# A planned attention and gating kernel: port-exclusive planning, output weights' words in PSUM, and batch 1's sums of v by matmuls

## The chip, the cores and the metric

The kernel runs on one core of one Trainium2 chip. The metric is the device time of one execution in microseconds (us). Times of the kernel before are 701.80, 700.61 and 698.42 us in three runs, with a median of 700.61 us.

The core has five engines that work side by side, each through its own list of instructions in a fixed order: TensorE (PE, matmuls; PEld is its loading of weights), VectorE (DVE), ScalarE (ACT), GpSimd (POOL) and SyncE (SP), which here only issues transfers. SBUF is the working memory. PSUM holds the results of matmuls; the kernel uses it as two score tiles (`sc`, 1024 floats a partition) and four banks of 512 floats (`acc`).

## The reference

Two stages, the second on the output of the first.

```python
# stage 1: B=4, H=8, S=768, D=64, 16 clusters
q_assign = argmax(q_n @ c_n)          # normalized, per head; the same for k
scores = where(q_assign == k_assign, q @ k.T / 8, -1e9)
attn = softmax(scores); x = attn @ v  # heads side by side: x is (4, 768, 512)
# stage 2: d_ff = 1024, halves u and v
h = relu(x @ w_in); u, v = h[..., :512], h[..., 512:]
v_n = (v - mean(v)) / sqrt(var(v) + 1e-6)
v_s = w_spatial @ v_n + b_spatial[:, None]
out = (u * v_s) @ w_out
```

`w_in` and `w_out` arrive as 64-bit floats. The kernel loads them as pairs of 32-bit words and puts a 32-bit float together from each pair with shifts and masks.

## The kernel before, in words

**Precision.** Products run in fp16 with a high and a low part of each operand, so that three matmuls stand for one: high by high, high by low, low by high. The high part is a scaled copy (mostly ACT), the low part a subtraction (DVE or POOL).

**Tiling.** Two heads make a pair; there are four pairs in each of four batches, so 16 pairs, n = 0 to 15. A batch's four pairs are followed by its gating stage.

- `prep(n)` loads q, k (`raw`) and v (`vraw`), forms `hq` (high parts, L532) and `lo` (low parts, L534), the logits against the centroids (L549 to L551), the one-hot assignments (L562 to L574), which a DMA transposes (`oht`, L580) and four DMAs put into `hq` as extra rows (L596), the high and low parts of v (`vhl`, L597 and L598), and the sums of v over the sequence, whose two rows go to `mean` (L622 to L626). For batch 0 (n < 4) the sums come from twelve matmuls of `ones` with `vhl` (L605, L606); for the others from a reduction of `vraw` on VectorE (L613) and a small fp32 matmul (L614).
- `shifts(n)` takes, per head, the largest score of each query: score matmuls into an `acc` bank (L654), a maximum over each (L661), then `nl` (L672), three columns on ACT (L673, L676), a DMA transpose `sht` (L677) and a DMA that puts three rows into `hq` (L678).
- `attend(n)` runs, for each of 12 tiles (6 a head), the scores (L698, L700), the exponential (L704), its fp16 copy (L706), its low part on POOL (L707) and 18 matmuls with v (L712). At a head's end the sum is divided (L731 to L733) and split into two parts (L735 on ACT, L736 on POOL).
- `mlp(b)` has six tiles of v (12 matmuls with `w_in`, ReLU on ACT at L777, mean and variance at L783 to L794, normalized at L796 to L798), six of u (L807), six products with `w_spatial` (18 matmuls, then L817 to L819 and a DMA transpose `gT`) and six with `w_out` (12 matmuls, L827). All these matmuls are issued at L756.
- The weights are converted once. `w_in` goes early, in eight jobs of 512 columns; its words are put together in `acc` banks, since its `tops` argument is that ring. `w_spatial` (12 jobs, plain fp32) and `w_out` (8 jobs of 256 columns) go later, when `w_in` is done. The words of `w_out` are put together in an SBUF tile `top` by three DVE instructions (L477, L478, L479); then come a high part on ACT (L461) and a low part on DVE (L462).

**What sets the order.** No order is written by hand. `Plan.op` collects every operation with its engine, a cost in us, what it depends on and a key. `Plan.run` then plays the program through with these costs. It always takes the engine that can start soonest, and on it, among the operations that are ready by then, the one with the smallest due time plus key. In that order the instructions are written into each engine's list. A ring (`Ring`) hands out buffers in turn, or, for `acc` and `sc`, by which comes free first. The numbers at the top of the file (`DUE`, `W_KEY`, `K_SC` and so on) are due times and keys. They take part in nothing but this choice.

Of the kernel before, what the change touches and what calls it, by code (L numbers as in the profile page):

```python
# [7 lines left out]
F32 = mybir.dt.float32  # L8
# [7 lines left out]
P = 128  # L16
# [4 lines left out]
P_LOG = 10  # L21
# [19 lines left out]
DUE_0 = 41.19  # L41
DUE = 25.06
DUE_PREP = -1.8
DUE_MAX = -0.66
DUE_M = 36.0
DUE_W = 1.18
# [6 lines left out]
W_KEY = 5.9  # L53
WL_KEY = 1.71
WL_AT = 183.82
WL_GAP = 3.25
W_AT = 31.81
W_GAP = 5.28
PREP_KEY = 2.74
AV_KEY = 0.83  # L60
K_SC = -2.21
K_MX = -3.21
K_MAX = -0.23

# [56 lines left out]
class Op:  # L121
    __slots__ = ("eng", "cost", "fn", "after", "order", "new", "claim", "key", "at", "dma", "turn", "cols", "due", "left", "ready", "outs", "end", "seq", "alt", "s", "free")
# [7 lines left out]
OVER = {"PE": 0.0, "ACT": 0.1, "DVE": 0.083, "POOL": 0.04, "SP": 0.0, "NONE": 0.0}  # L130

# [5 lines left out]
class Plan:  # L137
# [12 lines left out]
    def op(self, eng, cost, fn, after=(), use=(), new=(), claim=(), key=0.0, at=0.0, dma=None, turn=False, cols=0, alt=None, due=None):  # L150
        o = Op()
        o.due = self.due if due is None else due
# [9 lines left out]
    def run(self):  # L162
# [19 lines left out]
        hw = [0.0, 0.0]  # L182
        lanes = []
# [26 lines left out]
        while done < len(self.ops):  # L210
# [29 lines left out]
            if o.dma is None:  # L240
# [11 lines left out]
                o.end = s + c  # L252
                free[e] = o.end - OVER[e]
# [22 lines left out]
def kernel(  # L276
# [76 lines left out]
    r_top = R(wk, "top", [P, 256], F32, 1)  # L353
# [49 lines left out]
    def fill():  # L403
# [4 lines left out]
    c_wt = op("DVE", 1.2, fill, key=-8)  # L408
    c_id = op("DVE", 0.2, lambda: V.tensor_copy(out=id16, in_=idt()), after=[ld_i], use=[scratch], key=0)
    c_z = op("DVE", 0.5, lambda: (V.memset(cmh, 0.0), V.memset(cml, 0.0)), key=-8)  # L410
    c_oh = op("POOL", 1.0, lambda: (G_.memset(ohx, 0.0), G_.memset(ohx.rearrange("p t (x e) c -> p t x (e c)", e=2)[:, :, 0:2, C:C + 1], PEN)), key=-8)
    c_sh = op("POOL", 2.0, lambda: [G_.memset(x, 0.0) for x in shx], key=-7)
    c_mean = op("POOL", 0.6, lambda: [G_.memset(x, 0.0) for x in mean], key=-6)
    c_wh = op("POOL", 0.5, lambda: (G_.memset(one32, 1.0), [G_.memset(x[:, :, D:D + 1], S * MEAN_UNIT) for x in whs], [G_.memset(x[:, :, D:D + 1], 0.0) for x in wls]), key=-5)
    c_one = op("POOL", 0.8, lambda: [G_.memset(x[:, :, :, D:D + 1], 1.0) for x in vhl], key=-9)
    o = chain("DVE", [
        (0.1, lambda: V.tensor_tensor(out=sq(), in0=cn(0), in1=cn(0), op=ALU.mult)),
        (0.1, lambda: V.tensor_reduce(out=ss, in_=sq(), axis=AX.X, op=ALU.add)),
# [21 lines left out]
    c_cm = op("DVE", 1.0, place_c, after=[o, c_z], use=[ct], key=KC)  # L440
# [11 lines left out]
    def weights(jobs, at, gap, key, raws, tops, on, after=()):  # L452
        ends = []
        for m, (src, dst, n, lg, wide, cell) in enumerate(jobs):
# [4 lines left out]
            def lows(x, ld, n=n, dst=dst, sc=sc, raw=raw, cell=cell, use=()):  # L459

                h = op("ACT", 0.2 + 0.00085 * n, lambda: A.activation(out=dst()[:, 0, :], in_=x(), func=AF.Copy, scale=sc), after=ld, use=use, key=key)  # L461
                lo = op("DVE", (0.05 if n > 384 else 0.4) + 0.00125 * n, lambda: V.scalar_tensor_tensor(out=dst()[:, 1, :], in0=x(), scalar=sc, in1=dst()[:, 0, :], op0=ALU.mult, op1=ALU.subtract), after=[h], use=use, key=key)  # L462
                w_ops.setdefault(cell, []).extend([h, lo])
                ends.append(lo)
# [434 lines left out]
```

## Time and profile before

| what | value |
|---|---|
| times of three runs | 701.80, 700.61, 698.42 us |
| span of the profiled execution, first to last instruction | 696.3 us |
| median of the runs less that span | 4.3 us |
| mean granted TensorE clock | 0.993 |
| PE busy | 632.9 us, 91% |
| DVE busy | 480.1 us, 69% |
| ACT busy | 431.6 us, 62% |
| POOL busy | 427.4 us, 61% |

The page gives no time of the profiled execution's own beside its span, so the median less the span stands for what lies around it. Busy time is the time in which at least one instruction of an engine ran. Instructions of one engine overlap a little, and the ends of matmuls are modelled, so a busy PE is not a PE at its peak. "Idle before" in a row is the idle time of the engine just before such instructions, with what ended it. Lines are those of the kernel before; the changed file has the same code four lines lower from L355 on.

### The profile page before, as it was taken

The numbers are of one execution on the slowest core, as the hardware profiler recorded it, in microseconds if no ns is written. First come the engines' busy times: TensorE is split into PE (matmuls) and PEld (weight loads), VectorE is DVE, ScalarE is ACT, GpSimd is POOL, SyncE is SP. The second block draws the span as 40 slices with busy tenths as digits, with TensorE's granted clock in tenths as the row PEclk, the third lists the DMA queues.
The fourth block names the chain that finished last, engine by engine and source line by source line (L and its number), as shares of the span: only waits on it lengthen the run. The fifth ranks groups of instructions, "written<-read, shape, count | busy, mean of one in ns | idle before, by whom it ended". The sixth has DMA issues, their size and how long they took to land.

```text
span 696.3 us, 16724 instructions
## 1 busy us (share of the span) xinstructions
PE 632.9 (91%) x6751; PEld 374.0 (54%) x6751; DVE 480.1 (69%) x945; ACT 431.6 (62%) x679; POOL 427.4 (61%) x301
## 2 busy tenths in 40 slices
PE   2578789989899798999999999999999899989996
PEld 1245556656545455556555656556655556544442
DVE  6979999998976999978496858557586812015210
ACT  2359899988856856748773848558664855522111
POOL 1038698998756856847666857758575967613210
PEclk9999999999999999999999999999999999999999
DMA  5585664857342658283532437446410122230123
GB/s 163 138 220 129 176 151 89 166 123 143 87 126 61 141 151 183 69 194 73 150 76 54 108 46 120 105 107 106 112 30 1 37 43 54 49 96 1 31 60 91
DMA packets 107321, 70.69 MB, mean 102 GB/s; under 512 B 91182, under 2 KB 93932, under 8 KB 107244
## 3 DMA queue, kind: packets, MB, share of 16 engines
q1 hardware_dynamic: 103500, 62.94, 40.8%
q10 hardware_dynamic: 3744, 6.69, 2.8%
q8 instruction: 53, 0.87, 0.5%
q14 instruction: 24, 0.20, 0.1%
HBM read 27.63 MB, written 6.29 MB: 49 GB/s over the span
## 4 chain that ended last, share of the span: by engine, by line
PE 60%; DVE 24%; ACT 6%; DMA 6%; issue 3%; POOL 1%; SPq 0%; ACTq 0%; DVEq 0%; POOLq 0%
PE acc L756 35%; DVE nm L661 10%; PE acc L712 10%; PE sc L698 5%; PE sc L700 5%; PE acc L654 4%; ACT p L704 2%; ACT pt L706 2%; DMA gT<-ghl 2%; DMA sht<-shx 1%; DMA raw<-in_kqT_dram 1%; DVE lo L534 1%; DVE vhl L598 1%; POOL pt L707 1%; DVE wsp L462 1%
## 5 line engine op out<-in xcount | busy, mean ns | idle before, releaser
L707 POOL TENSOR_TENSOR pt<-p,pt 128x768 f16<-128x768 f32 x192 | 325.1, 1710 | 110.7 <-ACT pt L706 86.9
L704 ACT ACTIVATE p<-sc,plog 128x768 f32<-128x768 f32 x192 | 169.2, 898 | 43.4 <-PE sc L700 39.5
L661 DVE TENSOR_REDUCE nm<-acc 128x1 f32<-128x512 f32 (+1 forms) x288 | 178.7, 682 | 5.2 <-PE acc L654 4.9
L706 ACT CAST pt<-p 128x768 f16<-128x768 f32 x192 | 155.6, 830 | 7.6 <-PE acc L712 5.9
L712 PEld LDWEIGHTS <-pt 128*128 128x128 f16 x3456 | 125.6, 98 | 27.5 <-POOL pt L707 7.7
L712 PE MATMUL acc<-vhl,pt 128*128 128x65 f16 (+1 forms) x3456 | 134.6, 194 | 6.2 <-POOL pt L707 6.0
L756 PE MATMUL acc<-win,xT 128*128 128x512 f16 x576 | 130.0, 380 | 0.0
L654 PE MATMUL acc<-hq 80*128 80x256 f16 (+1 forms) x384 | 101.2, 338 | 19.0 <-DVE nm L661 10.1
L698 PE MATMUL sc<-hq,lo 128*128 128x512 f16 (+1 forms) x384 | 95.8, 331 | 6.4 <-ACT p L704 6.2
L700 PE MATMUL sc<-hq 81*128 81x512 f16 (+1 forms) x384 | 96.1, 332 | 4.4 <-DMA hq<-sht 4.4
L756 PE MATMUL acc<-vn,wsp 128*128 128x512 f16 x432 | 97.1, 379 | 0.1
L756 PEld LDWEIGHTS <-xT 128*128 128x128 f16 x576 | 55.1, 98 | 64.0 <-issue 1.7
L817 DVE SCALAR_TENSOR_TENSOR u<-acc,bsp,u 128x512 f32<-128x512 f32 x24 | 18.0, 749 | 92.3 <-PE acc L756 92.3
L819 POOL TENSOR_TENSOR ghl<-u,ghl 128x512 f16<-128x512 f32 x24 | 28.8, 1199 | 73.4 <-DVE ghl L818 65.8
L756 PE MATMUL acc<-wou,gT 128*128 128x512 f16 x288 | 65.8, 379 | 4.3 <-DMA gT<-ghl 4.3
L756 PEld LDWEIGHTS <-wsp 128*128 128x128 f16 x432 | 41.6, 98 | 48.5 <-issue 0.2
L654 PEld LDWEIGHTS <-hq 80*128 80x128 f16 x384 | 34.5, 99 | 42.0 <-issue 21.7
L700 PEld LDWEIGHTS <-hq 81*128 81x128 f16 x384 | 37.9, 99 | 31.3 <-issue 6.3
L698 PEld LDWEIGHTS <-lo 128*128 128x128 f16 x384 | 34.2, 98 | 34.7 <-issue 19.7
L534 DVE SCALAR_TENSOR_TENSOR lo<-raw,hq 128x768 f16<-128x768 f32 x32 | 41.7, 1305 | 15.7 <-ACT hq L532 15.6
L756 PEld LDWEIGHTS <-gT 128*128 128x128 f16 x288 | 27.5, 97 | 36.8 <-DMA gT<-ghl 5.8
L827 ACT ACTIVATE o<-acc 128x512 f32<-128x512 f32 x24 | 14.3, 596 | 48.9 <-PE acc L756 34.9
(104 smaller groups left out, 619.1 us busy)
## 6 DMA issues: line engine op xcount, KB each, us to landing
raw<-in_kqT_dram SPq DMA_DIRECT2D x15, 768.0 KB
vraw<-in_vp_dram SPq DMA_DIRECT2D x16, 384.0 KB
out_dram<-o ACTq DMA_DIRECT2D x24, 256.0 KB
hq<-hq SPq DMA_DIRECT2D x15, 384.0 KB
vn<-in_w_in_dram SPq DMA_DIRECT2D x8, 512.0 KB
hq<-lo SPq DMA_DIRECT2D x16, 192.0 KB
lo<-hq SPq DMA_DIRECT2D x16, 192.0 KB
wraw<-in_wsT_dram SPq DMA_DIRECT2D x12, 192.0 KB
```

Source lines behind the costliest of these rows:

```text
L534: los.append(op("DVE", 1.4 if n else 0.96, lambda h=h: V.scalar_tensor_tensor(out=lo.t[:, h, :], in0=raw.t[:, h, :], scalar=QK_SCALE, in1= ...
L654: T.matmul(out=acc.t[:, c:c + cs.stop - cs.start], lhsT=hq.t[0:R_SH, 1, h, t * P:(t + 1) * P], rhs=hq.t[0:R_SH, 0, h, cs], start=c == 0, s ...
L661: V.tensor_reduce(out=nm.t[:, t, k:k + 1] if n == 1 else nm.t[:, t:t + n, k], in_=src, axis=AX.X, op=ALU.max, negate=True)
L698: T.matmul(out=sc.t[:, cs], lhsT=lo.t[:, h, ks], rhs=hq.t[:, 2, h, cs], start=True, stop=False)
L700: T.matmul(out=sc.t[:, cs], lhsT=hq.t[0:R_E, 0, h, ks], rhs=hq.t[0:R_E, 1, h, cs], start=False, stop=True)
L704: o = op("ACT", 0.9, lambda sc=sc, p32=p32: A.activation(out=p32.t, in_=sc.t[:, 0:S], func=AF.Exp, bias=plog, scale=SC_UNIT), after=[o, m_ ...
L706: o = op("ACT", 0.83, lambda pt=pt, p32=p32: A.copy(out=pt.t[:, 0, :], in_=p32.t), after=[o], use=[p32], new=[pt], key=K_HI)
L707: o = op("POOL", 1.72, lambda pt=pt, p32=p32: G_.tensor_tensor(out=pt.t[:, 1, :], in0=p32.t, in1=pt.t[:, 0, :], op=ALU.subtract), after=[o ...
L712: T.matmul(out=av.t[:, t * (D + 1):t * (D + 1) + w], lhsT=lhsT, rhs=rhs, skip_group_check=True, **f)
L756: T.matmul(out=acc.t, lhsT=lr[m][0], rhs=lr[m][1], start=(m == 0), stop=(m == n - 1))
L817: o = op("DVE", 0.72, lambda: V.scalar_tensor_tensor(out=u32.t, in0=acc.t, scalar=bsp[:, t:t + 1], in1=u32.t, op0=ALU.add, op1=ALU.mult), ...
L819: l = op("POOL", 1.2, lambda: G_.tensor_tensor(out=ghl.t[:, 1, :], in0=u32.t, in1=ghl.t[:, 0, :], op=ALU.subtract), after=[h], use=[u32, g ...
```

## The change

Four things change.

1. **The planner gets a lock.** An operation may be marked `lock`; every POOL operation that is not a transfer is. While the plan is played, one number, `port`, holds the time until which the last locked operation runs, and a locked operation ends no sooner than that time, less 0.13, plus its cost. Marked on DVE are operations whose operands lie in SBUF alone: `lo` (L534), the copies of `hq` (L536), the low part of v (L598), the small statistics and the normalization (L789 to L797), `ghl` (L818), and the low parts of weights that come straight from `raw` (L462).
2. **Costs and keys are new.** Costs of DVE, ACT and POOL operations are other numbers (POOL's low part of the exponential 1.65 instead of 1.72, `lo` 0.94 instead of 1.4, the small statistics 0.16 instead of 0.3), and so are the due times and keys at the top. Costs, due times and keys move instructions; they change none.
3. **The words of `w_out` go to `acc` banks.** The ring `top` in SBUF is gone; `late_weights` passes `r_acc`, and a job uses the first 256 columns of a bank.
4. **The sums of v of batch 1** (n = 4 to 7) come from the twelve matmuls, as in batch 0, instead of L613 and L614.

Apart from points 3 and 4, each engine has the same instructions as before, in another order.

```diff
-DUE_0 = 41.19
-DUE = 25.06
+DUE_0 = 42.99
+DUE = 23.281
...
-DUE_M = 36.0
-DUE_W = 1.18
+DUE_M = 37.729
+DUE_W = 0.985
...
-WL_KEY = 1.71
-WL_AT = 183.82
-WL_GAP = 3.25
+WL_KEY = 5.317
+WL_AT = 181.201
+WL_GAP = -7.18
...
+PORT = 0.13
...
+        o.lock = dma is None and (lock or eng == "POOL")
...
+        port = 0.0
...
                 o.end = s + c
+                if o.lock:
+                    o.end = port = max(s, port - PORT) + c
                 free[e] = o.end - OVER[e]
...
-    r_top = R(wk, "top", [P, 256], F32, 1)
...
-            x1 = op("DVE", (0.1 if n > 256 else 0.3) + 0.0011 * n, lambda raw=raw, top=top, n=n: V.tensor_scalar(out=top.t.bitcast(U32), in0=words(raw, n, 1), scalar1=3, scalar2=0x3FFFFFFF, op0=ALU.logical_shift_left, op1=ALU.bitwise_and), after=[ld], use=[raw], new=[top], key=key)
+            x1 = op("DVE", 0.1 + 0.00113 * n, lambda raw=raw, top=top, n=n: V.tensor_scalar(out=top.t[:, 0:n].bitcast(U32), in0=words(raw, n, 1), scalar1=3, scalar2=0x3FFFFFFF, op0=ALU.logical_shift_left, op1=ALU.bitwise_and), after=[ld], use=[raw], new=[top], key=key)
...
-            lows(lambda top=top: top.t, [x3], use=[top])
+            lows(lambda top=top, n=n: top.t[:, 0:n], [x3], use=[top], lock=False)
...
-        weights(jobs, WL_AT, WL_GAP, WL_KEY, r_wraw, r_top, "SP", after)
+        weights(jobs, WL_AT, WL_GAP, WL_KEY, r_wraw, r_acc, "SP", after)
...
-        short = n >= NPR
+        short = n >= 2 * NPR
...
-                o = op("POOL", 1.72, lambda pt=pt, p32=p32: G_.tensor_tensor(out=pt.t[:, 1, :], in0=p32.t, in1=pt.t[:, 0, :], op=ALU.subtract), after=[o], use=[p32, pt], key=K_LO)
+                o = op("POOL", 1.65, lambda pt=pt, p32=p32: G_.tensor_tensor(out=pt.t[:, 1, :], in0=p32.t, in1=pt.t[:, 0, :], op=ALU.subtract), after=[o], use=[p32, pt], key=K_LO)
```

Three places show what the new plan moves. Numbers in the names tell buffers apart.

**ACT, around the 63rd to the 66th exponential (pair 5), while the gating stage of batch 0 begins.** `v` at L777 (L781 after) and `u` at L807 (L811 after) take in a tile of twelve matmuls with `w_in`. Before:

```order
L597 ACTIVATE vhl_89<-vraw 128x12x64
L704 ACTIVATE p_3013<-sc_111,plog 128x768
L704 ACTIVATE p_3042<-sc_110,plog 128x768
L706 CAST pt<-p_3013 128x768
L706 CAST pt<-p_3042 128x768
L735 CAST xhl<-xn 128x6x64
L704 ACTIVATE p_3097<-sc_111,plog 128x768
L532 ACTIVATE hq<-raw 128x768
L706 CAST pt<-p_3097 128x768
L704 ACTIVATE p_3136<-sc_110,plog 128x768
```

Now:

```order
L739 CAST xhl<-xn 128x6x64
L710 CAST pt<-p_2941 128x768
L710 CAST pt<-p_2961 128x768
L811 ACTIVATE u_3013<-acc_113 128x512
L708 ACTIVATE p_3065<-sc_111,plog 128x768
L708 ACTIVATE p_3091<-sc_110,plog 128x768
L710 CAST pt<-p_3065 128x768
L628 ACTIVATE wl_95<-w_3101 2x2x65
L710 CAST pt<-p_3091 128x768
L781 ACTIVATE v_3166<-acc_113 128x512
```

Before, the third tile with `w_in` follows the 71st exponential. Now a tile of u follows the 62nd and the third tile of v the 64th, so 24 matmuls with `w_in` stand earlier in PE's list.

**DVE, the first two jobs of `w_out`, between the shifts of pair 7 and those of pair 8.** Before:

```order
L477 TENSOR_SCALAR top<-wraw 128x256
L732 RECIPROCAL rc<-rc 128x6
L534 SCALAR_TENSOR_TENSOR lo<-raw,hq 128x768
L733 TENSOR_TENSOR xn<-acc_114,rc 128x384
L817 SCALAR_TENSOR_TENSOR u_3313<-acc_115,bsp,u_3313 128x512
L622 TENSOR_SCALAR wh_93<-acc_113 2x2x64
L478 SCALAR_TENSOR_TENSOR top<-wraw,top 128x256
L623 SCALAR_TENSOR_TENSOR w_4086<-acc_113,wh_93 2x2x64
L818 CAST ghl<-u_3313 128x512
L479 SCALAR_TENSOR_TENSOR top<-wraw,top 128x256
L462 SCALAR_TENSOR_TENSOR wou<-top,wou 128x256
L477 TENSOR_SCALAR top<-wraw 128x256
```

Now:

```order
L822 CAST ghl<-u_3013 128x512
L481 TENSOR_SCALAR acc_113<-wraw 128x256
L578 TENSOR_SCALAR ohx<-acc_115 128x6x2x16
L482 SCALAR_TENSOR_TENSOR acc_113<-wraw,acc_113 128x256
L481 TENSOR_SCALAR acc_115<-wraw 128x256
L483 SCALAR_TENSOR_TENSOR acc_113<-wraw,acc_113 128x256
L482 SCALAR_TENSOR_TENSOR acc_115<-wraw,acc_115 128x256
L538 SCALAR_TENSOR_TENSOR lo<-raw,hq 128x768
L821 SCALAR_TENSOR_TENSOR u_3416<-acc_114,bsp,u_3416 128x512
L735 TENSOR_SCALAR rc<-acc_112 128x6
L483 SCALAR_TENSOR_TENSOR acc_115<-wraw,acc_115 128x256
```

The words now stand in the banks `acc_113` and `acc_115`, and two jobs are open at once, where before one tile `top` served one job after the other.

**SP, the first shift of pair 0.** Before:

```order
L538 DMA hq<-hq 64x2x1536
L580 DMA_TRANSPOSE oht<-ohx 128x6x128
L677 DMA_TRANSPOSE sht<-shx_86 128x6x128
L472 DMA vn<-in_w_in_dram 128x1024
L596 DMA hq<-oht 17x768 x2
L678 DMA hq<-sht 3x768
L596 DMA hq<-oht 16x768 x2
```

Now:

```order
L542 DMA hq<-hq 64x2x1536
L681 DMA_TRANSPOSE sht<-shx_86 128x6x128
L584 DMA_TRANSPOSE oht<-ohx 128x6x128
L476 DMA vn<-in_w_in_dram 128x1024
L682 DMA hq<-sht 3x768
L600 DMA hq<-oht 17x768 x2
L600 DMA hq<-oht 16x768 x2
```

The transpose for pair 0's shift goes ahead of that for pair 1's one-hot rows, and its rows are written before theirs.

More of the change, by code (lines that the diff above doesn't have):

```diff
@@ L121 @@
 class Op:
-    __slots__ = ("eng", "cost", "fn", "after", "order", "new", "claim", "key", "at", "dma", "turn", "cols", "due", "left", "ready", "outs", "end", "seq", "alt", "s", "free")
+    __slots__ = ("eng", "cost", "fn", "after", "order", "new", "claim", "key", "at", "dma", "turn", "cols", "due", "left", "ready", "outs", "end", "seq", "alt", "s", "free", "lock")
 LAG = {"PE": 0.2, "ACT": 0.034, "DVE": 0.034, "POOL": 0.034, "SP": 0.0, "NONE": 0.0}
@@ L148, in ring, with op @@
         return r
-    def op(self, eng, cost, fn, after=(), use=(), new=(), claim=(), key=0.0, at=0.0, dma=None, turn=False, cols=0, alt=None, due=None):
+    def op(self, eng, cost, fn, after=(), use=(), new=(), claim=(), key=0.0, at=0.0, dma=None, turn=False, cols=0, alt=None, due=None, lock=False):
         o = Op()
+        o.lock = dma is None and (lock or eng == "POOL")
         o.due = self.due if due is None else due
@@ L438, in place_c @@
             V.tensor_tensor(out=cml[r, :, i, :], in0=ctv[r], in1=cmh[r, :, i, :], op=ALU.subtract)
-    c_cm = op("DVE", 1.0, place_c, after=[o, c_z], use=[ct], key=KC)
+    c_cm = op("DVE", 1.25, place_c, after=[o, c_z], use=[ct], key=KC)
     w_ops = {}
@@ L776, in v_tile @@
             k = t % 2
-            o = op("ACT", 0.57, lambda: A.activation(out=v32.t, in_=acc.t, func=AF.Relu, scale=2.0 ** -(X_LOG + WIN_LOG)), after=[o], use=[acc], new=[v32], key=K_VT)
+            o = op("ACT", 0.596, lambda: A.activation(out=v32.t, in_=acc.t, func=AF.Relu, scale=2.0 ** -(X_LOG + WIN_LOG)), after=[o], use=[acc], new=[v32], key=K_VT)
             if k == 0:
@@ L792, in v_tile @@
[L792 to L794 removed]
+            o = op("DVE", 0.165, lambda: V.tensor_scalar(out=a.t, in0=mv.t[:, :, 1], scalar1=1e-6, scalar2=None, op0=ALU.add), after=ags, use=[mv], new=[a], key=0, lock=True)
@@ new lines, in v_tile @@
+            o = op("POOL", 0.69, lambda: G_.tensor_tensor(out=y.t, in0=a.t, in1=mhalf.broadcast_to([P, 2]), op=ALU.pow), after=[o, m_half], use=[a], new=[y], key=-2)
+            o = op("DVE", 0.16, lambda: V.tensor_tensor(out=y2.t, in0=y.t, in1=y.t, op=ALU.mult), after=[o], use=[y], new=[y2], key=0, lock=True)
+            o = op("DVE", 0.16, lambda: V.tensor_tensor(out=y2.t, in0=y2.t, in1=a.t, op=ALU.mult), after=[o], use=[y2, a], key=0, lock=True)
+            o = op("DVE", 0.16, lambda: V.tensor_scalar(out=y2.t, in0=y2.t, scalar1=-0.5 * 2.0 ** VN_LOG, scalar2=1.5 * 2.0 ** VN_LOG, op0=ALU.mult, op1=ALU.add), after=[o], use=[y2], key=0, lock=True)
@@ L799, in v_tile @@
+                l = op("POOL", 1.25, lambda t=t, v=v: G_.tensor_tensor(out=vn[:, 1, t, :], in0=v.t, in1=vn[:, 0, t, :], op=ALU.subtract), after=[h], use=[v], key=1)
                 normed.extend([h, l])
```

130 lines of the change are left out of this document (62 added, 68 removed).

## The prediction

> **What bounds the kernel now.** First the page's sums and its chain of waits, then the windows by stage, then the waits.
>
> ```profile
> span 696.3 us, 16724 instructions
> PE 632.9 (91%) x6751; PEld 374.0 (54%) x6751; DVE 480.1 (69%) x945; ACT 431.6 (62%) x679; POOL 427.4 (61%) x301
> PE 60%; DVE 24%; ACT 6%; DMA 6%; issue 3%; POOL 1%; SPq 0%; ACTq 0%; DVEq 0%; POOLq 0%
> ```
>
> PE is the bound over the whole, and VectorE holds a quarter of the chain. Where, the windows tell (each engine's busy us in the stretch, then the granted PE clock):
>
> ```profile
> 0.00:50.00 50.00, 25.14 (x221) 13.55 (x222) 38.80 (x102) 17.84 (x29) 6.84 (x20) 1.00 0.60 166
> 50.00:125.00 75.00, 64.40 (x991) 45.74 (x988) 72.67 (x137) 68.21 (x110) 63.17 (x40) 0.98 0.60 144
> 125.00:200.00 75.00, 66.91 (x893) 43.59 (x889) 70.91 (x124) 64.49 (x101) 65.02 (x42) 0.95 0.57 121
> 200.00:300.00 100.00, 92.87 (x1033) 54.89 (x1033) 88.27 (x165) 66.64 (x111) 64.06 (x40) 1.00 0.52 128
> 300.00:600.00 300.00, 294.57 (x3163) 175.13 (x3160) 186.55 (x364) 198.59 (x306) 205.26 (x141) 1.00 0.39 82
> 600.00:696.30 96.30, 89.00 (x474) 41.10 (x472) 22.91 (x58) 15.86 (x26) 23.04 (x21) 1.00 0.22 54
> ```
>
> The columns are PE, PEld, DVE, ACT, POOL. PE is idle for 24.9 us in the first 50, 10.6 to 125, 8.1 to 200, 7.1 to 300, 5.4 in the next 300 and 7.3 at the end. VectorE is busy 72.7 of 75 us, then 70.9 of 75, then 88 of 100, and after that 187 of 300. So the time is to be won before 300 us, where VectorE is nearly full; behind that PE runs through, and a shorter VectorE buys nothing.
>
> **The change, part by part.**
>
> *Batch 1's sums by matmuls.* What goes is a reduction on VectorE and a two-pass fp32 matmul, what comes is twelve fp16 matmuls. The rows of both: grouped, the waits, a piece of the chain, and in order of time:
>
> ```profile
> L613 DVE TENSOR_REDUCE vs<-vraw 128x128 f32<-128x768 f32 x12 | 17.8, 1487 | 0.2 <-DMA vraw<-in_vp_dram 0.2
> PE acc L614 <- DVE vs L613: 3.3, 3, 1.4
> 363.85 1.37 DVE vs L613
> 73.51 0.22 PE L605 MATMUL acc<-vhl,ones 128*128 128x130 f16 x1
> 74.15 0.22 PE L606 MATMUL acc<-vhl,ones 128*128 128x128 f16 x1
> 118.86 0.38 PE L614 MATMUL acc<-vs,one 128*2 128x128 f32 x2 [0.68 <-DVE vs L613]
> 119.17 0.39 PE L654 MATMUL acc<-hq 80*128 80x512 f16 x1
> ```
>
> VectorE loses 4 x 1.49 = 5.9 us of work. PE's twelve start from 73.51 to 74.15, and one more step of 0.06 makes 0.70; L614 takes 0.31 to the next start. So PE gains 4 x (0.70 - 0.31) = 1.6 us of work. Against it stands PE's wait for the reduction: 3.3 us in three, of which the 1.4 is at 364 us, in batch 2, and stays; the 1.9 goes. Net -0.3. The new chain has to wait for the low part of v, which the reduction did not. That is covered, as pair 4 shows, the tightest case:
>
> ```profile
> 126.89 1.57 DVE L598 SCALAR_TENSOR_TENSOR vhl<-vraw,vhl 128x768 f16<-128x768 f32 x1
> 151.31 0.34 PE L712 MATMUL acc<-mean,hq 83*128 83x65 f16 x6
> ```
>
> From 128.5 to the first use at 151.3 there are 22.8 us; if that cover were gone, it would cost the 0.70 us of the matmuls and a transfer a pair. The twelve wait themselves, though, and PE keeps its order: scores queued behind them then wait for a late low part, by at most the 1.57 us that a blocked one takes. The plan places them where it expects the low part to be there, so I count nothing. The 5.9 us on VectorE I count at nothing by themselves: they lie beside PE's work and show only in the order below.
>
> *Words of the output weights in PSUM.* The SBUF words (shortest, median and longest ns, first and last start; then mean ns), one of the same instructions on `w_in`, whose words already stand in a bank, and POOL's main work:
>
> ```profile
> L477 DVE TENSOR_SCALAR top<-wraw x8: 278/298/1618, 247.5 to 298.4; 128x256 uint32<-128x256 uint32 x8
> L478 DVE SCALAR_TENSOR_TENSOR top<-wraw,top x8: 403/722/1865, 250.0 to 298.7; 128x256 uint32<-128x256 uint32 x8
> L462 DVE SCALAR_TENSOR_TENSOR wou<-top,wou x8: 403/420/1590, 252.3 to 300.9; 128x256 f16<-128x256 f32 x8
> L478 DVE SCALAR_TENSOR_TENSOR top<-wraw,top 128x256 uint32<-128x256 uint32 x8 | 7.6, 952 | 0.1
> L479 DVE SCALAR_TENSOR_TENSOR top<-wraw,top 128x256 uint32<-128x256 uint32 x8 | 7.3, 918 | 0.1
> L477 DVE TENSOR_SCALAR top<-wraw 128x256 uint32<-128x256 uint32 x8 | 5.0, 625 | 0.1
> L462 DVE SCALAR_TENSOR_TENSOR wou<-top,wou 128x256 f16<-128x256 f32 x8 | 5.6, 700 | 1.6 <-ACT wou L461 1.6
> L478 DVE SCALAR_TENSOR_TENSOR acc<-vn,acc 128x512 uint32<-128x512 uint32 x8 | 5.3, 686 | 0.0
> L707 POOL TENSOR_TENSOR pt<-p,pt 128x768 f16<-128x768 f32 x192 | 325.1, 1710 | 110.7 <-ACT pt L706 86.9
> ```
>
> In SBUF one form takes 0.40 to 1.87 us; twice the size in a bank takes 0.69 on average, so those hardly wait for anyone. POOL's low part takes 1.71 us, and the longest extra, 1865 - 403 ns, stays under that. The new price of one instruction lies between 0.40 (the free case in SBUF) and 0.69 (512 columns); I take 0.42, since the form and the size are those of the first. The four cost 625 + 952 + 918 + 700 = 3195 ns now and 4 x 0.42 = 1.68 us then: 8 x 1.5 = 12 us of VectorE less (3 us at the upper bound), between 247 and 301 us.
>
> The Trainium skill (SBUF — State Buffer, "Who interferes with whom") states that a VectorE instruction with two SBUF inputs and a GpSimd instruction that reads SBUF exclude each other for a whole instruction; the spread of L478 agrees. Its page VectorE: DVE Perf Modes ("Why PSUM operands drop a tier") speaks against the change: L477, with one input, would lose its double rate in PSUM. The 278 ns of its quickest case beside 403 for the two-input form agrees; by that rule the 12 us would be 11.
>
> What of it reaches PE? In that stretch PE waits little, and mostly for a bank that VectorE's `u` product has yet to free, queued behind such words:
>
> ```profile
> 250.00:275.00 25.00, 22.61 (x274) 13.61 (x271) 23.20 (x37) 13.17 (x22) 15.32 (x10) 1.00 0.77 189
> 275.00:300.00 25.00, 24.34 (x295) 15.13 (x293) 24.90 (x48) 19.45 (x32) 17.22 (x11) 1.00 0.39 88
> PE acc L654 <- DVE u L817: 2.3, 1, 2.3
> ```
>
> PE is idle 2.4 and 0.7 us, so 3.1 is all that can come back here. I take -2.0; the other 10 us are off the path.
>
> *The order.* Two tiles with `w_in`, 24 matmuls, move up from behind the 71st exponential. Their price and the place they move to:
>
> ```profile
> 200.34 7.88 PE acc L756 x36
> 150.00:175.00 25.00, 23.48 (x331) 15.33 (x328) 21.88 (x38) 22.89 (x37) 22.18 (x15) 1.00 0.66 133
> 175.00:200.00 25.00, 21.55 (x224) 12.89 (x220) 24.95 (x42) 18.58 (x29) 20.27 (x14) 0.86 0.36 79
> 200.00:225.00 25.00, 25.00 (x236) 13.73 (x236) 15.16 (x40) 14.07 (x26) 12.21 (x9) 1.00 0.37 110
> 225.00:250.00 25.00, 20.91 (x238) 12.42 (x236) 25.00 (x45) 19.95 (x34) 19.30 (x13) 1.00 0.54 126
> ```
>
> A matmul is 7.88 / 36 = 0.219 us, so 5.3 us of PE work leave the block from 200 us on, where PE is full (25.00) and the others idle, and go where PE is idle 1.5 + 3.5 us and its granted clock is 0.86 of full over 25 us, another 3.5 us of PE time lost. Bounds: nothing, if pair 5's scores are pushed back by as much, and 8.5 us. I take -4.5, a little over half, because exponentials, copies and POOL there stand at 22 of 25 us and cannot close up much. Between 225 and 250 PE is idle 4.1 us while VectorE is full; 5.9 us of sums are gone from VectorE by then, but the weights of `w_spatial` still lie there: -1.0 (0 to -4.1).
>
> The clock's dip comes where PE is thinly used. The Trainium skill (TensorE: Matmul & The Clock Gate, Part 1) states that after a window of some 3.4 us with too little activity the clock is halved for at least as long; the 0.86 agrees with two such windows. If the thin stretch only moves (by its list PE still has no matmuls with `w_in` among the scores of pair 5's second head), so does the dip, which is why I do not count all 3.5.
>
> *The start.* Pair 0's shift rows are written before the one-hot rows of pair 1:
>
> ```profile
> 32.20 2.07 SPq L580 DMA_TRANSPOSE oht<-ohx  x1
> 38.01 0.70 SPq L678 DMA_DIRECT2D hq<-sht  x1
> PE sc L700 <- DMA hq<-sht: 4.4, 1, 4.4
> ```
>
> PE's longest wait, 4.4 us, ends with these rows. The transpose of 2.07 us that now goes ahead will not, so the first exponential may come up to 2 us sooner. But pair 1 follows VectorE, which is full from 50 to 75 us, and its own one-hot rows are now later by as much. I take 0 (bounds -2 and +2).
>
> *The rest.* From 300 us on no engine's list loses or gains work, and from the last matmuls with v to the end PE's list is the same sequence. Moved pieces there can cost or win within the 5.4 us that PE idles: 0. The lock itself costs the chip nothing; it is a number in the planner.
>
> **The sum.** -0.3 - 2.0 - 4.5 - 1.0 = -7.8 us against the profiled span: 696.3 becomes 688.5. The median of the runs lies 4.3 above that span, and I carry the difference over: 700.6 - 7.8 = 692.8, say 693.
>
> **The rivals.**
>
> *No change.* Up to 200 us the softmax's chain of exponential, copy and POOL's low part, at 22 to 23 of 25 us, paces every pair; more matmuls among the scores push the pair back, and PE idles later instead. For it: DVE, ACT and POOL are all around 90% busy there. Against it: the block from 200 us on, in which these three are at 12 to 15 of 25, would still be shorter. Without the order's -5.5 the sum is -2.3: 698.
>
> *Slower: four banks are too few.* A job's words hold a bank from the first word to the low part. A job's bank would have been held from 247.5 to past 252.3 with the first one, and two jobs are now open at once, beside the bank that collects a head's output, one for the logits and one for a tile of the gating stage. Maxima and gating tiles then wait for a bank, PE in its fixed order with them. The price is half a tile of twelve matmuls (6 x 0.219 = 1.3 us) for each of eight jobs, 10.5 us, which replaces the -2.0: 693 + 2 + 10.5 = 705. It decides from 1.2 us a job on, where it has eaten all of the gain (9.8 / 8). For it: the 2.3 us wait above is one for a bank. Against: all of PE's waits for maxima are short, those in the stretch where `w_in`'s words held banks included:
>
> ```profile
> PE acc L654 <- DVE nm L661: 10.1, 23, 1.6
> ```
>
> *More.* PE's idle time from 125 to 300 us, 15.2 us, goes down to the share of the later 300 us (1.8%, 3.2 us), and the clock's 3.5 comes back: -15: 685.5.
>
> *The planner's lock does not catch what the chip does*, so that its order is only another order, worth as much as any: no particular sign, within 4 us of before: 700.
>
> **How the numbers follow.** What a measurement of this kernel can tell from no change is about 0.5%, 3.5 us. Forecast, 688 to 697: 0.50. More, below 688: 0.11. No change or an order like any other, 697 to 704: 0.23. Banks or another stall, above 704: 0.16. The forecast's own range is 688 to 697; that of 8 in 10 is 686 to 705, where the lower end is the case "more" and the upper one the banks at their price. Faster 0.61, same 0.23, slower 0.16.
>
> **What would show it.** Right: the words at 0.42 us each with hardly a spread; PE idle in 150 to 200 us below 3 us, with pair 6's first scores some 5 us earlier than in this row; the same PE work from 300 us on, only sooner.
>
> ```profile
> 219.38 0.49 PE L698 MATMUL sc<-hq,lo 128*128 128x512 f16 x2
> ```
>
> For the banks: waits of PE for VectorE's `u` or maxima of more than 5 us in 240 to 300. For the pace: pair 5's and pair 6's exponentials as late as now. Wrong is the forecast if the stretch from 300 us on grows by more than 3 us, or if PE's idle time before 125 us, 35.5 now, moves by as much.

## The result

The changed kernel takes 679.37 us (median of four runs, 678.34 to 679.79), the kernel before 701.16 in the same comparison (four runs, 698.42 to 701.80). The ratio is 0.970, with a 95% interval of 0.968 to 0.972: 21.8 us faster. Two further executions of the kernel before and one of a run below took over 900 us at a granted clock of 0.67; ratios, intervals and the clock's loss in this document leave them out. Forecast was 693, so the sign was right, the size was not: the time lies below the forecast's range, and below the 686 of the range of 8 in 10 too. The head of the page after, and of its chain of waits:

```profile
span 677.3 us, 16827 instructions
PE 628.3 (93%) x6791; PEld 375.3 (55%) x6791; DVE 460.5 (68%) x941; ACT 433.3 (64%) x679; POOL 423.7 (63%) x301
PE 57%; DVE 26%; ACT 6%; issue 5%; DMA 4%; POOL 2%; SPq 0%; ACTq 0%; DVEq 0%; POOLq 0%
```

The span is 19.0 us shorter; PE's busy time fell by 4.6 us, VectorE's by 19.6. Every execution on record with both numbers takes 1.7 to 1.9 us more than its span. So of the 4.3 us by which the median of the kernel before lies above its profiled span, some 2.5 only mean that the profiled execution was a quick one; that is why the two spans differ by less than the medians. The windows by stage (PE, PEld, DVE, ACT, POOL, granted PE clock):

```profile
0.00:50.00 50.00, 26.59 (x249) 14.69 (x250) 42.32 (x109) 19.37 (x31) 8.87 (x21) 1.00 0.59 164
50.00:125.00 75.00, 65.20 (x1000) 46.12 (x997) 72.82 (x136) 70.08 (x111) 63.96 (x40) 0.95 0.70 156
125.00:200.00 75.00, 72.32 (x935) 47.50 (x932) 65.63 (x129) 66.29 (x108) 66.02 (x43) 1.00 0.59 135
200.00:300.00 100.00, 95.69 (x1089) 57.81 (x1088) 79.39 (x157) 66.75 (x110) 65.14 (x43) 1.00 0.61 141
300.00:600.00 300.00, 296.67 (x3203) 177.00 (x3201) 180.56 (x363) 199.46 (x303) 203.82 (x141) 1.00 0.35 76
600.00:677.30 77.30, 71.87 (x333) 32.18 (x330) 19.81 (x51) 11.34 (x19) 15.95 (x15) 1.00 0.21 48
```

PE's idle time fell from 8.1 to 2.7 us between 125 and 200, from 7.1 to 4.3 up to 300, from 5.4 to 3.3 in the next 300 and from 7.3 to 5.4 at the end. The dips of the clock between 125 and 200 us (0.95 before) are gone; between 50 and 125 us the clock stands a little lower than before (0.95 for 0.98). The longest of what PE waits for between 50 and 310 us (waits: us in all, times, longest), before and after:

```profile
PE sc L698 <- ACT p L704: 6.2, 9, 2.0
PE acc L654 <- DVE nm L661: 5.5, 16, 1.6
PE acc L712 <- POOL pt L707: 4.9, 8, 1.5
```

```profile
PE sc L702 <- ACT p L708: 3.2, 7, 1.2
PE acc L609 <- DVE xn L737: 2.1, 1, 2.1
PE acc L658 <- DVE nm L665: 2.1, 9, 0.4
PE acc L716 <- POOL pt L711: 1.8, 3, 0.9
```

The three long lists of short waits (exponentials, maxima, POOL's low part) shrank together, from 16.6 to 7.1 us. Single longer waits came and went: the 2.3 us for `u` that the prediction shows is gone, and 2.1 us at a sum of v (L609) are new. The words of the output weights, grouped, are as forecast, 0.42 us:

```profile
L481 DVE TENSOR_SCALAR acc<-wraw 128x256 uint32<-128x256 uint32 x8 | 3.3, 415 | 0.0
L482 DVE SCALAR_TENSOR_TENSOR acc<-wraw,acc 128x256 uint32<-128x256 uint32 x8 | 3.3, 420 | 0.1
```

And pair 6's first scores, with two bursts of the values' matmuls (in order of time):

```profile
206.27 1.25 PE L716 MATMUL acc<-vhl,pt 128*128 128x65 f16 x36
...
211.03 0.49 PE L702 MATMUL sc<-hq,lo 128*128 128x512 f16 x2
...
245.81 0.70 PE L716 MATMUL acc<-vhl,pt 128*128 128x65 f16 x18
```

They start at 211.03 instead of 219.38 us: 8.4 us had been won by then, and another 11 came later. The bursts tell why busy PE hides some of that: 36 matmuls take 1.25 us, 18 take 0.70, so one more costs 0.031, and about 0.15 us at a burst's end counts as busy without a new matmul starting (an estimate from these two rows; the ends of matmuls are modelled). By it a wait shorter than that between two bursts is no idle time on the page. The Trainium skill (Perfetto Trace Analysis, "Identifying the Most-Contended Engine") states that matmul busy time is a poor measure of how near PE is to its limit, because matmuls are pipelined; the two bursts agree.

### The profile page after: what moved, and what is told of

The parts are those of the page before. It is cut to its first block, busy times and chain, and to the rows that moved or that the text cites. A ratio compares the mean times of both kernels' runs of the same rounds, so it can differ in the third digit from the quotient of the medians.

```text
span 677.3 us, 16827 instructions
## 1 busy us (share of the span) xinstructions
PE 628.3 (93%) x6791; PEld 375.3 (55%) x6791; DVE 460.5 (68%) x941; ACT 433.3 (64%) x679; POOL 423.7 (63%) x301
## 4 chain that ended last, share of the span: by engine, by line
PE 57%; DVE 26%; ACT 6%; issue 5%; DMA 4%; POOL 2%; SPq 0%; ACTq 0%; DVEq 0%; POOLq 0%
PE acc L760 33%; DVE nm L665 11%; PE acc L716 9%; PE sc L702 5%; PE sc L704 5%; PE acc L658 4%; DMA gT<-ghl 3%; ACT p L708 2%; DVE lo L538 1%; ACT pt L710 1%; DVE vhl L602 1%; DVE acc L481 1%; POOL pt L711 1%; DVE acc L482 1%; DVE acc L569 1%
## 5 line engine op out<-in xcount | busy, mean ns | idle before, releaser
L716 PE MATMUL acc<-vhl,pt 128*128 128x65 f16 (+1 forms) x3456 | 132.6, 193 | 2.1 <-POOL pt L711 1.8
L658 PE MATMUL acc<-hq 80*128 80x256 f16 (+1 forms) x384 | 98.6, 336 | 11.0 <-DVE nm L665 6.0
L538 DVE SCALAR_TENSOR_TENSOR lo<-raw,hq 128x768 f16<-128x768 f32 x32 | 44.6, 1406 | 24.2 <-ACT hq L536 24.1
L811 ACT ACTIVATE u<-acc 128x512 f32<-128x512 f32 x24 | 14.3, 597 | 56.2 <-PE acc L760 50.3
```

What stands on the lines that cost most here:

```text
L538: los.append(op("DVE", 0.94, lambda h=h: V.scalar_tensor_tensor(out=lo.t[:, h, :], in0=raw.t[:, h, :], scalar=QK_SCALE, in1=hq.t[:, 0, h, ...
L658: T.matmul(out=acc.t[:, c:c + cs.stop - cs.start], lhsT=hq.t[0:R_SH, 1, h, t * P:(t + 1) * P], rhs=hq.t[0:R_SH, 0, h, cs], start=c == 0, s ...
L716: T.matmul(out=av.t[:, t * (D + 1):t * (D + 1) + w], lhsT=lhsT, rhs=rhs, skip_group_check=True, **f)
```

## The experiments

Where a run keeps an order, the planner's choice is replaced by a list of operation numbers, and its dependences stay:

```diff
+ORDER = [0, 10, 2, 3, 6, ...]
...
-            best = None
...
+            o = self.ops[ORDER[done]]
```

Three runs keep the list strictly: the new order with the old instructions, words back in SBUF and sums back to the reduction. In the other runs that keep an order, an operation that isn't ready in the play-through, or has no free buffer there, stands back until it is, so a few operations can move.

All results in one table. "Clock's loss" is the span times one less the granted clock, the median over a run's executions: an upper bound of what dips cost, since a dip costs nothing where PE would have waited. "Without it" is the span times the clock, so a lower bound. The kernel before, run beside each of the four groups of runs that follow, had medians of 698.9, 698.8, 700.1 and 700.8 us, and 701.2 beside the changed kernel. So a difference of medians between two groups, and one to the changed kernel's 679.4, can be off by some 2 us beyond the intervals.

| run | median us | ratio to before, 95% | clock's loss | without it |
|---|---|---|---|---|
| kernel before (77 executions in the four groups) | 698.8 to 700.8 | 1 | 7.0 to 9.1 | 690 to 691 |
| changed kernel | 679.4 | 0.970 (0.968 to 0.972) | 3.4 | 674.2 |
| new order, both old instructions | 693.0 | 0.991 (0.988 to 0.994) | 10.7 | 680.3 |
| old order, both new instructions | 703.1 | 1.006 (1.004 to 1.009) | 10.5 | 690.8 |
| planned without the lock | 693.6 | 0.992 (0.989 to 0.995) | 6.2 | 686.5 |
| planned with the old keys | 702.6 | 1.004 (1.002 to 1.007) | 14.0 | 686.4 |
| words back in SBUF | 687.1 | 0.983 (0.978 to 0.988) | 8.9 | 676.4 |
| sums back to the reduction | 686.3 | 0.982 (0.977 to 0.987) | 6.2 | 679.2 |
| start undone | 680.7 | 0.974 (0.969 to 0.980) | 3.7 | 675.8 |
| tiles back | 689.5 | 0.986 (0.982 to 0.990) | 7.2 | 680.8 |
| three undone | 702.9 | 1.005 (1.002 to 1.007) | 15.4 | 685.9 |
| old order, tiles up | 703.1 | 1.006 (1.003 to 1.008) | 10.5 | 691.1 |
| old order, instructions placed | 697.9 | 0.998 (0.996 to 1.000) | 7.0 | 689.6 |
| old order, all three | 701.1 | 1.002 (1.000 to 1.005) | 9.8 | 689.4 |
| old order to pair 4, then new | 686.3 | 0.980 (0.976 to 0.984) | 4.1 | 679.8 |
| new to pair 4, then old | 697.5 | 0.996 (0.993 to 0.998) | 9.0 | 686.2 |
| new to pair 6, then old | 691.8 | 0.989 (0.985 to 0.993) | 11.0 | 679.9 |
| old to pair 8, then new | 697.8 | 0.997 (0.995 to 0.999) | 8.4 | 688.3 |

### Order and instructions apart

**New order, old instructions.** The changed kernel's order, words in SBUF (two buffers), sums by the reduction ahead of the low part of v.

```diff
+    r_top = R(wk, "top", [P, 256], F32, 2)
-        weights(jobs, WL_AT, WL_GAP, WL_KEY, r_wraw, r_acc, "SP", after)
+        weights(jobs, WL_AT, WL_GAP, WL_KEY, r_wraw, r_top, "SP", after)
-        short = n >= 2 * NPR
+        short = n >= NPR
```

> The order of the changed kernel, kept operation by operation, with the instructions of the kernel before: words of the output weights in SBUF (two buffers) and batch 1's sums by the reduction, put in front of the low part of v. Theory A (the order carries the gain, the instructions little): 679 to 685 us, at least three quarters of the 21.8 us between 701.2 and 679.4 remain. Theory B (VectorE's work, 18 us less by the rows, carries it): 692 us or more. By my sum of before, the instructions alone are worth 2.3 us, so 682.

**Old order, new instructions.** The kernel before's order, with both new instructions; the sums' matmuls stand right behind the low part of v that they need.

```diff
-        weights(jobs, WL_AT, WL_GAP, WL_KEY, r_wraw, r_top, "SP", after)
+        weights(jobs, WL_AT, WL_GAP, WL_KEY, r_wraw, r_acc, "SP", after)
-        short = n >= NPR
+        short = n >= 2 * NPR
```

> The reverse: the order of the kernel before, kept but for a few operations that a bank not yet free, or the sums' wait for the low part of v, moves back, with the words in PSUM banks and batch 1's sums by matmuls. Theory A: 696 to 702 us. Theory B: 690 us or less. If the four banks are too few in an order that was not made for them: above 703, with waits of PE for VectorE between 240 and 300 us.

**Without the lock**, and **with the old keys**: the changed kernel, planned anew.

```diff
-        o.lock = dma is None and (lock or eng == "POOL")
+        o.lock = False
```

> The changed kernel, planned anew with the lock left out of the planner; costs, due times, keys and instructions as changed. Theory A1 (the lock makes the order fit the chip): half of the gain or more is lost, 690 us or more. Theory A2 (the keys make the order, and the lock only moves planned times): 678 to 685 us.

```diff
-DUE_0 = 42.99
-DUE = 23.281
...
+DUE_0 = 41.19
+DUE = 25.06
...
```

> The changed kernel, planned anew with the due times and keys of the kernel before; lock, costs and instructions as changed. Theory A1 (lock and costs suffice): 678 to 687 us. Theory A2 (the keys make the order): 690 us or more.

The new order alone gives 5.9 us of the 21, the new instructions alone lose 4.2: they are worth 13.6 us in the new order and less than nothing in the old. A reason for the loss stands in the waits between 110 and 235 us of the old order with new instructions; the run "instructions placed" below takes it away:

```profile
PE acc L723 <- DVE vhl L715: 4.4, 3, 1.5
```

Three times PE stands 1.5 us at a sum, for the low part of v, with the next scores queued behind. In the new order with the old instructions, the clock dips where PE becomes thin (two windows, clock 0.88 and 0.87):

```profile
225.00:250.00 25.00, 23.36 (x323) 16.04 (x323) 23.74 (x43) 20.89 (x36) 20.52 (x13) 0.88 0.45 89
250.00:275.00 25.00, 20.33 (x172) 11.00 (x171) 22.95 (x39) 9.11 (x17) 10.76 (x8) 0.87 0.60 137
```

Without the lock, 14 us of the gain are lost, and with the old keys all of it. But each is another plan as a whole, one of many that such numbers give. That the lock helps because it foresees the port is not shown by this.

### One part undone in the changed kernel

**Words in SBUF** and **sums by the reduction**, each the edit above alone.

> The changed kernel with every engine's order kept, only the words of the output weights back in SBUF, with two buffers so that two jobs may still be open at once; the sums of v stay matmuls. With both old instructions this order took 693.0 us, with both new ones 679.4; this run and the next share out the 13.6 us. Theory A (the port: in SBUF the words wait for POOL and POOL for them, between 225 and 300 us, where VectorE is full): most of it comes back, 687 to 691 us, lost between 225 and 300 us, with nothing lost by pair 4's first scores (139 us). Theory B (what counted in the first run was the reduction, already before 143 us): 680 to 682 us. By the prediction's terms (2.0 for the words): 681.

> The changed kernel with every engine's order kept, only batch 1's sums of v back to one reduction on VectorE and one two-pass matmul a pair, the reduction just ahead of the low part of v; the words stay in PSUM. Theory A: VectorE has 4 x 1.5 us more before 225 us, and the run that undid both had lost 3.5 us by pair 4's first scores; the rest was the words: 682 to 684 us. Theory B: 688 to 692 us, since the delay before 143 us is handed on and grows. By the prediction's terms (0.3): 680. If the two parts add up, this run and the one with words in SBUF lose 13.6 us together; if less, each hides the other.

Words: 7.7 us slower. PE's waits from 225 to 300 us, a window there, and the second word:

```profile
PE acc L773 <- DVE u L936: 2.9, 1, 2.9
PE acc L773 <- ACT u L926: 1.7, 1, 1.7
```

```profile
250.00:275.00 25.00, 20.41 (x198) 12.27 (x197) 22.13 (x38) 14.05 (x25) 13.32 (x9) 0.93 0.60 150
```

```profile
L597 DVE SCALAR_TENSOR_TENSOR top<-wraw,top x8: 407/426/1261, 239.6 to 279.6; 128x256 uint32<-128x256 uint32 x8
```

In SBUF this word takes up to 1.26 us again (0.64 on average, by its group's row), in a bank 0.42; the rule of exclusion that the prediction cited from the Trainium skill (SBUF — State Buffer, "Who interferes with whom") agrees. The four steps of a job take 633 + 642 + 535 + 847 ns on average here and 415 + 420 + 417 + 415 in the changed kernel, so VectorE has 7.9 us more to do. VectorE's `u` comes late, PE waits 2.9 and 1.7 us for maxima tiles whose bank is not free, and the clock dips (0.93 of 25 us, 1.8 us). Before, the same wait was 2.3 us.

Sums: 7.0 us slower. PE's waits from 110 to 235 us, in this run and in the changed kernel:

```profile
PE acc L772 <- DVE nm L779: 3.3, 10, 0.7
PE acc L732 <- DVE nm L779: 2.4, 3, 1.2
```

```profile
PE acc L658 <- DVE nm L665: 1.0, 4, 0.4
```

The reduction itself is hardly waited for (0.2 us). The maxima stand behind it in VectorE's list, and PE waits for those, ten times at their own matmuls and three times at the sums' small matmul (L732). The two runs together lose 14.7 us, the run that undid both 13.6: the parts add up within the intervals, and each of theory A and B had half of it.

**The start undone.** SP's list:

```diff
-L681 hq<-sht ahead of L584 oht<-ohx (the change)
+L584 oht<-ohx and two rows of hq<-oht ahead of L681 sht and L682 hq<-sht
```

> The changed kernel with the start's two transfers back as they were: the one-hot rows of pair 1 are transposed and written before pair 0's shift rows; nothing else moves. By the prediction's term: 0, so 679 us, since pair 1 follows VectorE. By the traces of both kernels (first exponential 42.74 us before, 41.38 after, and pairs 1 to 3 earlier by 2.2 to 2.7 us): 1.4 us later at the first exponential and 1.4 to 2.7 us at the end, 681 to 682 us.

The median is 1.3 us higher, by the ratios to the kernel before 3 us (0.974 for 0.970), and the two intervals overlap. The profiled span is the same (677.2 and 677.3): pair 4's first scores come 1.2 us later (140.3 for 139.1), pair 7's second head is level (262.2 and 262.4). So the profile is with the term of 0, but the times can't tell it from the 1.4 to 2.7 us of the other reading.

**The two tiles back.**

```diff
  exponential 62
-u 0: 12 matmuls with w_in, ReLU
  exponential 64
-v 2: 12 matmuls with w_in, ReLU, statistics
  ...
  exponential 71
+u 0, v 2
```

> The changed kernel with the two tiles with w_in (24 matmuls, with their ReLU or statistics) back behind the 71st exponential, where they stood before; all else in its order. By the prediction's term for them, 4.5 us: 684 us, with PE thin between 150 and 200 us again. Rival 1 (the tiles only fill time in which PE would have waited anyway, and give no more than their own 5.3 us of PE work): at most 685. Rival 2 (the softmax's chain paces these pairs, and moving the tiles wins nothing): 679 to 680. If the thin stretch brings a dip of the clock too, up to 3.5 us more: 687.

10.1 us slower, twice the term. Two windows of this run, then of the changed kernel:

```profile
150.00:175.00 25.00, 21.81 (x318) 15.22 (x318) 18.17 (x33) 22.46 (x37) 21.77 (x15) 0.97 0.62 153
175.00:200.00 25.00, 21.54 (x195) 12.45 (x194) 15.22 (x29) 14.85 (x23) 15.23 (x11) 0.89 0.35 87
```

```profile
150.00:175.00 25.00, 24.21 (x335) 16.43 (x333) 19.08 (x35) 22.75 (x38) 22.52 (x16) 1.00 0.64 160
175.00:200.00 25.00, 24.15 (x219) 13.69 (x218) 22.32 (x49) 18.95 (x33) 18.61 (x13) 1.00 0.49 110
```

PE idles 5.0 us more (6.65 for 1.64) and loses 3.5 us to the clock (0.03 and 0.11 of 25 us): 8.5 of the 10.3 us by which pair 6's first scores are late here (221.3 for 211.0). In the new order the tiles fill time that PE would have idled, and the clock stays up with them.

### The same parts put into the old order

**Three undone** is the control: the changed order with both old instructions and the tiles back, the edits above together.

> The changed kernel's order with three parts undone at once: words in SBUF with two buffers, batch 1's sums by the reduction, and the two tiles with w_in back behind the 71st exponential. If the parts add up (13.6 us for both instructions, 10.1 for the tiles): 703 us, as slow as the kernel before, and nothing else in the order carries any gain. If the parts are paid for by the same idle time: 695 to 699.

702.9: they add up, and without them the new order gains no time. It has the largest clock's loss of all runs, though; with that set aside it stands at 685.9 us, the kernel before at 690 to 691. So the three parts looked like the whole change. The other three runs put them into the old order.

**Tiles up:** in the old order u 0 and v 2 move from behind the 71st exponential to where the change has them. Their matmuls follow the 62nd and the 64th exponential, as in the change; the ReLU of v 2 follows the 67th here (64th there), and v 1 stays behind the 62nd, where the change has it behind the 60th.

> The kernel before with its order kept and only the two tiles with w_in (24 matmuls and what follows them) moved up to where the change has them, behind the 62nd to 66th exponential. By the prediction's term, 4.5 us: 696.5. If they are worth here what moving them back cost in the changed kernel, 10.1 us: 691, with the two dips of the clock between 184 and 198 us gone. If they only pay in the new order: 699 to 702.

**Instructions placed:** words in PSUM and sums by matmuls, each sum as many operations behind the low part of v as in the change (6 to 20).

```diff
  low part of v
-sums of v
  ... 6 to 20 operations
+sums of v
```

> The kernel before with its order kept, words in PSUM and batch 1's sums by matmuls, but these matmuls placed as far behind the low part of v as the change places them (in the run at 703 us they stood right behind it, and PE waited 1.5 us three times for it). If that wait is what the 703 us came from: 4.4 us and some clock less, 694 to 698. If the two instructions are worth in this order what they are worth in the new one (13.6): 687. If they are worth nothing without the new order: 700 to 703.

**All three:** both edits together.

> The kernel before with its order kept and the three parts put in by hand: words in PSUM, sums by matmuls placed as in the change, the two tiles moved up. If the three parts are the whole gain: 677 to 681 us. If the rest of the new order carries a share of its own, or each part needs it: 686 to 694.

The gain is not there: 703.1, 697.9 and 701.1 us against 700.1. The windows of "tiles up" show where the tiles' 5.3 us went:

```profile
150.00:175.00 25.00, 23.94 (x325) 15.45 (x322) 22.04 (x41) 22.95 (x38) 22.25 (x15) 1.00 0.61 127
175.00:200.00 25.00, 21.44 (x231) 12.97 (x230) 20.81 (x38) 17.95 (x26) 18.42 (x14) 0.96 0.32 68
200.00:225.00 25.00, 24.13 (x214) 12.61 (x213) 19.40 (x41) 14.24 (x27) 12.07 (x10) 0.90 0.41 120
```

PE is idle 3.6 us from 175 to 200, as before (3.4). Pair 5's second head is pushed back by 3.0 us (186.7 for 183.7), and the clock dips 25 us later (0.96 and 0.90 instead of 0.86). Pair 6's first scores start at 219.8 us, before at 219.4. What PE waits for from 150 to 215 us, here and in the changed kernel, is above all maxima that are late:

```profile
PE acc L772 <- DVE nm L779: 3.5, 8, 1.2
```

```profile
PE acc L658 <- DVE nm L665: 0.4, 2, 0.2
```

In the kernel before these waits were 3.4 us, so the tiles took none of them away. The instructions placed are worth 2.2 us here, where the sums had 1.5 us of PE's wait each otherwise. So each of the three parts costs 7 to 10 us when it is taken out of the new order and brings 2 at most when it is put into the old one. And the rest of the new order gains nothing without the three parts (702.9), the three parts nothing without the rest (701.1): the 21.8 us need both.

### Four cuts between the two orders

The old order with all three parts (701.1 us) and the change's order hold the same instructions, so what differs between them is the rest of the order. Each run takes one up to a pair's first exponential and the other from there on.

```diff
+pre = OLD[:OLD.index(first exponential of pair 4)]
+ORDER = pre + [x for x in NEW if x not in pre]
```

> The changed kernel's instructions, with the order of the run at 701 us (the old order with the three parts put in) until pair 4's first exponential, and the change's order from there on. In that run pair 4's first scores came 5.2 us behind the changed kernel. If that delay is handed on and the rest of the new order works by itself: 684 to 686 us. If the new order behind pair 4 only works with its own head start: 690 to 700. If nothing before pair 4 counts: 679.

> The opposite cut: the change's order until pair 4's first exponential, then the old order with the three parts put in. If the 5.2 us gained by then are handed on: 696. If they are lost again in the old order's waits behind it: 699 to 703. With the cut before, the two shares should make 22 us if they add up.

> The change's order until pair 6's first exponential, then the old order with the three parts put in. At pair 6's first scores the run at 701 us was 9.2 us behind the changed kernel: 691 to 693 if this is handed on, so pairs 4 and 5 carry about 4 us and what comes after pair 6 another 13. By the prediction, which put nearly all of the order's gain between 150 and 225 us: 683 or less.

> The old order with the three parts put in until the first exponential of pair 8's second head, near 320 us, then the change's order. By the prediction, nothing is to be won from 300 us on: 700 to 702. By the idle time of PE and the dips of its clock behind 300 us (7.8 us in the run at 701, 3.4 in the changed kernel): 696 to 698.

New to pair 4 wins 3.7 us (701.1 to 697.5), new from pair 4 on 14.9 (701.1 to 686.3): together 18.5 of 21.8, and the missing 3.3 lie within the intervals. (Seen from the other side, 686.3 to 679.4, what lies before pair 4 is worth 6.9.) Pairs 4 and 5 win 5.6 (697.5 to 691.8). Behind pair 8's first head the new order wins 3.3 (701.1 to 697.8). What is left, 21.8 - 3.7 - 5.6 - 3.3 = 9.2, lies in pairs 6 to 8. Each share is uncertain by 2 to 3 us by the intervals. The waits of PE from 50 to 310 us, in the old order with all three, old to pair 4, and new to pair 4:

```profile
PE acc L829 <- POOL pt L824: 8.3, 13, 1.5
PE acc L771 <- DVE nm L778: 6.9, 17, 1.2
```

```profile
PE acc L834 <- POOL pt L829: 6.8, 10, 1.5
...
PE acc L776 <- DVE nm L783: 2.7, 10, 0.4
```

```profile
PE acc L776 <- DVE nm L783: 8.5, 19, 1.6
...
PE acc L834 <- POOL pt L829: 3.1, 5, 0.9
```

The waits go with the stretch. Where the old order runs before pair 4, PE waits for POOL's low part (6.8 and 8.3 us against 1.8 in the change); where it runs behind pair 4, it waits for maxima (8.5 and 6.9 against 2.1). Exponentials go with the first: 6.3 and 5.7 us where the old order runs before pair 4, 3.8 and 3.2 where the new one does.

## Why the prediction was wrong

**The step that failed is the pricing of the order: "-4.5 and -1.0", from one moved piece and two windows of the kernel before, with 0 for the start and 0 from 300 us on, added to the terms of the two instructions as if each stood alone.** With the three parts in both, the rest of the order is worth 21.8 us, spread over four stretches at 4 to 7, 6, 9 and 3 us; without them it is worth nothing. What it takes away are many short waits of PE, for POOL's low part and exponentials before pair 4 and for maxima behind it. With all of the clock's loss set aside it is 689.4 to 674.2, still 15.2 us; so at most 6.6 us of it go with the clock. The signs set for "right" came true (words at 0.42 us, PE idle below 3 us from 150 to 200, pair 6's first scores 8.4 us earlier): they watched only the places that had been priced.

- *Sums by matmuls, -0.3.* Undone in the changed kernel: 7.0 us. The two terms of it (twelve short matmuls; the wait for the reduction) were right but small. What was "counted at nothing", 5.9 us on VectorE, is by the waits what counted, with the maxima queued behind. The risk that was named, a blocked sum at up to 1.57 us, is real: 1.5 us, three times, in the old order. In the change no sum of batch 1 waits for it.
- *Words, -2.0.* Their price of 0.42 us held, and so did the 12 us on VectorE: 3195 - 1667 ns in eight jobs. (That 12 would be 11 by the loss of L477's double rate is counted twice: at 0.42 it was in the 12.) In the old order words and placed sums together bring 2.2 us (interval 0.1 to 3.2), against -2.3 forecast. Undone in the new order the words cost 7.7, of which 2.2 at least remain without the clock's loss. "3.1 is all that can come back here" was read off the kernel before: it says for what the old order waits there, not what another order loses when the words are slow.
- *The tiles, -4.5.* The mechanism holds in the new order: PE's idle time from 150 to 200 us is 1.6 us (below 3 was forecast), and the dips are gone. The size is 10.1, as the clock's 3.5, which the -4.5 held only in part, came back whole. In the old order the rival "no change" had the mechanism right: more matmuls pushed pair 5 back by 3 us, and PE idled as before. Between the two, by the waits, stand the maxima: PE waits for them for 3.5 us from 150 to 215 us in the old order with the tiles up, for 0.4 in the change. No run moves the maxima alone.
- *Start, 0*: borne out by the profile, not settled by the times. (PE's longest wait was not the 4.4 us named there: 6.6 us for the clusters, at L431, stand before it, and 7.1 in the change.) *The rest, 0*: wrong by 4 to 7 us before pair 4 and 3 behind 300 us. PE's idle time before 125 us moved only from 35.5 to 33.2, under the bound of 3 that I had set, and pair 4's first scores still came 4.6 us earlier (139.1 for 143.7), half of it between 125 and 140 us. So the criterion, too, looked at the wrong quantity.
- *The rivals.* Banks: from 225 to 300 us PE waits for no `u` and no maxima of more than 1 us. The stall that this rival feared came once: 18 matmuls with `w_spatial` wait at 241.9 us for the low part of a word job to free its bank (first row below), behind a `lo` that takes 2.38 us on VectorE. That is one such wait, not the eight at 1.3 us that the rival was priced at. "More" (whose own terms make 15.5 us, not 15) came nearest, at a chance of 0.11: PE's idle time from 125 to 300 us went to 7.0, not 3.2, and the rest came from stretches it left out. The lock: planned without it, the kernel is 14 us slower, but with `lo` at 1406 ns on average after and 1305 before, it does not take the contention away, and whether it foresees it better stays open.

```profile
PE acc L760 <- DVE wou L466: 1.5, 1, 1.5
```

```profile
L534 DVE SCALAR_TENSOR_TENSOR lo<-raw,hq 128x768 f16<-128x768 f32 x32 | 41.7, 1305 | 15.7 <-ACT hq L532 15.6
```

```profile
L538 DVE SCALAR_TENSOR_TENSOR lo<-raw,hq 128x768 f16<-128x768 f32 x32 | 44.6, 1406 | 24.2 <-ACT hq L536 24.1
```

Which of the new keys make the short waits shrink together is not settled by these runs, and why the parts and the rest of the order need each other is read from the waits, not tested.

## What to carry to other kernels

An edit has no price of its own when the whole order is planned anew with it: the same three parts were worth 23.5 us in one order (702.9 to 679.4) and nothing in another, so a sum of parts priced in the old trace says little of the whole. Count the short waits by kind over the whole stretch in which an engine is nearly full (here PE's for maxima, exponentials and low parts, 16.6 us), and add the dips of the clock; in this case a new order won more than half of these waits (9.5 us) and some of the dips, and the idle time of the windows in which something visibly moves told too little. And put work that waits on another engine some operations behind what it waits for: twelve matmuls, 0.7 us in all, cost 1.5 us of waiting three times when they stood right behind it.

## What the runs showed of the hardware

The granted clock differs between executions of the same kernel, and the time goes with it. The 77 executions of the kernel before have mean clocks from 0.984 (six, spans of 700.0 us on average) to 0.995 (eight, 695.2). Fitted over all 77, a us of the clock's loss goes with 0.63 us of span (standard error 0.07; 0.52 to 0.92 in the four groups by themselves). By that slope, an estimate, about 3 of the 21.8 us are fewer dips: the loss is 7 to 9 us before and 3.4 after. With the three parts undone it is 15.4. In these runs a thin stretch on PE is paid for twice, as idle time and then at half the clock (0.50 below); the sum of the prediction had priced the second only in part.

The dips come without a long wait. In the run with the tiles back, where 3.5 us go to the clock from 150 to 200 us, PE's longest wait in that stretch is the first row; the other two are the stretch ahead of the first dip, with PE busy for 0.85 of 3.00 us, and the dip itself (clock 0.50):

```profile
PE acc L834 <- POOL pt L829: 1.5, 1, 1.5
```

```profile
170.00:173.00 3.00, 0.85 (x20) 0.63 (x17) 2.82 (x9) 3.00 (x6) 1.45 (x2) 1.00 0.88 185
174.00:176.00 2.00, 2.00 (x27) 1.12 (x24) 2.00 (x3) 0.06 (x1) 2.00 (x2) 0.50 0.97 358
```

The Trainium skill (TensorE: Matmul & The Clock Gate, "HAM oscillation — how this bites in real kernels") gives as a rule that PE should have no idle gaps above some 3.4 us. Here the dips came with gaps of 1.5 us at most, among short bursts; the measurement decides, and that rule does not say how thin is too thin.
